# The opening of a fused attention-and-MLP kernel in a new order: first value products before first key products, value weights loaded earlier

## The chip, the cores and the metric

The kernel runs on one core of one Trainium2 chip. The metric is the device time of one execution in microseconds (us). The core has five engines that run at the same time, each through its own queue in order: TensorE (PE in the profile, its weight loads are PEld), VectorE (DVE), ScalarE (ACT), GpSimd (POOL) and SyncE (SP), which here only issues DMA transfers.

## The reference

One block with two halves over x, 2048 tokens by 512 features, in bfloat16. `c` is a condition vector; `mod` holds six vectors of 512 made from it.

```python
mod = (silu(c) @ w_mod)            # sa, ca, ga, sb, cb, gb
h = layernorm(x) * (1 + ca) + sa
q, k, v = h @ wqkv                 # 32 heads of 16
pq, pk = q @ w_phi, k @ w_phi      # per head, 16 x 16
phi_q = concat(softmax(pq), softmax(-pq)); phi_k likewise
kv = sum over tokens of phi_k^T v;  z = sum over tokens of phi_k
o = (phi_q @ kv) / (phi_q . z + 1e-6)
x = x + ga * (o @ wo)
h = layernorm(x) * (1 + cb) + sb
x = x + gb * ((sigmoid(h @ w_gate) * (h @ w_up)) @ w_down)
```

The sums kv and z run over all 2048 tokens, so no token's attention output can start before the last token's key features are in.

## The kernel before, in words

The tokens are 16 tiles (0 to 15) of 128. All weights stay in on-chip memory. `w_phi` is folded into the query and key weights, so that one product per tile gives pq or pk. The program is a graph of 1230 named tasks. Each task has an engine and issues one or a few instructions. One long string, `ORDER` (line 39 on), names every task once; a name may carry `@A`, `@D` or `@P`, which puts it on ACT, DVE or POOL. The string is emitted from front to back, so it sets the order of each engine's queue and, through the slots that it hands out, which buffer and which of the eight PSUM banks a task gets. Nothing reorders it later: an instruction that waits holds all that stands behind it in its queue.

The names that are needed below, with the lines of their instructions:

- `ld_x0a`, `ld_x0b`, `ld_x1a` and so on (L537, on SP) load two tiles of x each, 256 KB: x0a tiles 0 and 1, x0b 2 and 3, x1a 4 and 5, x1b 6 and 7, x2b 10 and 11; `ld_x3a` loads tiles 12 to 15. `ld_wk0`, `ld_wk1` (L545) load the halves of the key weights, 256 KB each. `ld_wm00a/b` and `ld_wm01a/b` (L542) load the four pieces of `w_mod` for sa and ca, 256 KB each: wm00 for the features of blocks 0 and 1, wm01 for blocks 2 and 3. `ld_wv0` (L551) loads the value weights, 512 KB.
- `st1_t` (L702 and L703, DVE) takes mean and variance of tile t; `rs1_g` (L709/L710 on ACT, L712/L713 on POOL) the inverse root for a group of one or two tiles; `nmr1_g` (L718, DVE) mean times it; `xn1_t` (L731 POOL, L729 DVE) normalizes; `tphgj` (L744, PE) transposes block j of group g.
- `c1`, `c2`, `c3` make silu(c). `modc1.0` and `modc1.1` (L630, PE) multiply it with wm00 and wm01, and `modc1c0` (ACT) and `modc1c1` (L638, DVE) copy the results out. `hm1_gj` (L751 ACT, L753 DVE or POOL) applies (1 + ca) and sa to block j of group g. Blocks 0 and 1 need modc1c0, blocks 2 and 3 need modc1c1. The result is `h1T`.
- `tpw`, `wTc`, `fold1`, `foldc1` (L661, L664, L679, L685) fold the key weights; `warm` (L600) are matrix products of zeros.
- `Kt` (L817) and `Vt` (L821) are the key and value products, four matmuls of 512 columns; the first ones are cut in halves `a` (blocks 0, 1) and `b` (blocks 2, 3). `et` (L776, ACT) takes both exponentials, `nt` (L780, DVE) their sums, `rt` (L794/L795 ACT, L798 DVE) the reciprocals, `phit` (L787, DVE or POOL) the features, `vat` (L836) copies the values out, and `kvt` (L282, PE) adds to the sums. `qe`, `qn`, `qphi` (L784) are the same for the queries.
- `kvn0`, `kvn1` (L294) and `kvz0`, `kvz1` (L299), on DVE, mask the finished sums. They wait for every `kvt`. After them come `num` (L326) and the attention output, the second normalization and the MLP, whose products (L447, L485) fill TensorE to the end.

[...]

Of the kernel before, what the change touches and what calls it, by code (L numbers as in the profile page):

```python
# [43 lines left out]
K1a hm1_20@A ld_x2a hm1_12 hm1_02@A wqT1 ld_x3a tph03 xn1_4 hm1_23 hm1_13@A tph41 st1_8 hm1_03@A hm1_41@A st1_9 K0a hm1_22@A rs1_6@P tph43 hm1_43@A tph40 K1b
rs1_5@P K0b ld_wv0 wqT3 tph30 tph33 tph32 K2a tph42 hm1_40 wqT2 fold01 hm1_33 tph31 nmr1_6 K2b ld_wmga st1_14 hm1_30@A xn1_11 e0.0 hm1_31@A wqT0 xn1_10 xT1_11
K3a xT1_10 K3b foldc01 nmr1_5 xn1_8 V3a st1_15 e3.0 V0a rs1_8@P e2.0 V0b V3b fold03 va3 foldc03 ld_wmm2 V2a st1_12 n0.0 V2b xn1_9 fold02 nmr1_8 r0.0@A hm1_32
modca.0 va0 foldc02 modca.1 tph50 n2.0 xn1_15 modcac hm1_50 n3.0 e1.0 xn1_14 phi0.0 hm1_60@P V1a V1b hm1_62@P K4a hm1_63@P fold00 tph82 tph52 K4b foldc00
r2.0@A va1 va2@D r3.0@A Q0 st1_13 rs1_7@P hm1_82@A n1.0 hm1_42@A kv0.0 Q2 Q1 r1.0@A phi3.0@D phi2.0@D modc2.0 qe0.0 modc2.1 nmr1_7 qe2.0 ld_wo xn1_12 phi1.0@D
tph51 qe1.0 modc2c xn1_13 qn0.0 e4.0 kv1.0 qn2.0 hm1_52 kv2.0 Q4 K5a kv3.0 xT1_12 xT1_13 qphi0.0@P qphi0.1@P qn1.0 qe4.0 qphi2.1 tph80 K5b hm1_80@A hm1_51@A
e5.0 pT0 qphi2.0 n4.0 r4.0@A qn4.0 n5.0 phi4.0@D qphi1.1@P hm1_61@P qphi1.0@P tph53 V5 K7a V4 va5 hm1_53@A V6 pT2 hm1_70@P qphi4.1 va4 hm1_71 mask4 va6 K6a  # L50
K7b K6b e6.0 K8 tph83 hm1_83 r5.0 qphi4.0@P e8.0 pT1 pT4 ld_wd2 tph81 hm1_81 n6.0 n8.0 e7.0 n7.0 V7 kv4.0 hm1_72@P K11 K9 V9 K14 V8 r6.0@A e9.0 va7 va9 r7.0@A
e11.2 e11.6 phi5.0 phi6.0 hm1_73@P n9.0 r9.0@A kv5.0 gwa gra gwb e11.4 e14.0 K10 phi7.0@D kv6.0 K12 V10 kv7.0 e14.4 r8.0 n11.6 n11.2 r11.6 phi9.0 e10.0 e12.0
ld_wd ld_wu0 grb n11.4 n14.0 r11.2 n14.4 r14.0 n10.0 r14.4@A phi8.0 va8 V11 V14 n12.0 e11.0 K13 n11.0 phi11.6 r11.4 wo1 r11.0 va10 r10.0@A va11 kv8.0 kv9.0
phi11.2@D phi11.0@D phi10.0@D phi11.4@D V12 K15 e13.0 wmod_free ld_wg0 phi14.4 phi14.0 kv10.0 kv11.4 kv11.6 Q6 kv11.0 e13.4 r12.0@A e15.4 n13.0 n13.4 r13.0
r13.4 n15.4 e15.0 va14 V15 V13 qe6.0 va12 kv11.2 n15.0 r15.0 r15.4@A va13 phi13.4 Q5 phi15.4 phi13.0@D va15 phi15.0@D phi12.0@D wo0 wo3 Q3 kv12.0 kv13.0
kv14.0 kv15.0 qn6.0 kvn0 kvz0 kv13.4 kv14.4 kv15.4 kvz1 kvn1 num0a num1a num2a wo2 rd0a wo_all rd1a qe3.0 u0a num0b num4a num1b rd0b Q11 qe5.0 rd2a u0b u2a
rd4a num2b qn3.0 u1a rd1b tpo0 Q8 qphi6.0@P qphi6.1@P oT0 out0 num4b rd2b u1b wd0 qe11.0 u2b qphi3.1@P qphi3.0@P x1_0 rd4b st2_0 qe8.0 Q7 qe7.0 tpo1 oT1 Q10
Q9 out1 Q15 oT2 rs2_0 qn5.0 nmr2_0 xn2_0 u4a u4b x1_1 qn7.0 tsw xnT0 out2 qphi5.1@P qphi5.0@P pT6 mod02 mod00 qphi7.0@P pT3 mod03@A mod01@A qe15.0 qphi7.1@P
Q13 g0.8 x1_2 tg0.8 g0.1 st2_1 wd1 rs2_1 tg0.1 u0.8 u0.1 g0.0 num3b g0.4 hm0.1 hm0.8 pT5 qe9.0 tg0.4 g0.9 wd2 u0.4 u0.9 rd3b u3b tg0.9 g0.5 num3a hm0.4 hm0.9
u0.2 u0.0 num6a tg0.5 tg0.0 rd3a u3a u0.5 g0.2 hm0.0 hm0.5 rd6a nmr2_1 qe10.0 tg0.2 oT4 g0.10 u0.10 wd6 hm0.2 g0.3 pT7 tg0.3 u6a g0.6 num6b u0.3 y0.0 y0.1  # L60
rd6b tg0.10 hm0.10 hm0.3 num5a num5b u6b rd5b wd3 wd4 wd5 oT3 oT6 xn2_1 qe13.0 tg0.6 rd5a y0.2 u5b g0.7 tg0.7 out4 u5a oT5 qn11.0 u0.6 u0.7 xnT1 num7a hm0.6
hm0.7 mod13@A mod12@A rd7a x1_4 y0.3 out3 qphi11.1@P qphi11.0@P x1_3 st2_3 out6 mod10@A mod11@A g1.2 tg1.2 g1.1 tg1.1 num7b wd7 u1.3 u1.2 hm1.2 u7a g1.4 u1.1
y0.4 rd7b hm1.1 u1.4 y0.5 tg1.4 hm1.4 g1.0 g1.10 u1.10 g1.3 u7b st2_2 rs2_2 tg1.10 tg1.3 hm1.10 hm1.3 pT11 out5 tg1.0 u1.7 g1.7 x1_6 nmr2_2 u1.0 hm1.0 g1.5
u1.5 x1_5 qn10.0 wd8 y0.6 g1.6 oT7 xn2_2 xn2_3 g1.8 y0.7 Q14 y0.8 wd10 tg1.7 tg1.5 hm1.5 out7 u1.8 u1.6 st2_4 tg1.6 xnT2 xnT3 wd9 x1_7 qphi10.0 Q12 hm1.7
st2_6 mod21@P mod20@P qphi10.1@P y1.0 pT10 tg1.8 mod22@A mod23@A hm1.6 g1.9 y1.1 y1.2 tg1.9 u1.9 y0.9 y1.3 y1.4 g2.5 y0.10 g2.6 st2_5 qe12.0 st2_7 hm1.8 qn9.0
tg2.5 qe14.0 rs2_4 hm1.9 rs2_3 nmr2_4 y1.5 u2.0 g2.1 g2.0 tg2.0 xn2_7@D hm2.0 nmr2_3 fin0 y1.6 g2.2 tg2.2 u2.6 u2.2 hm2.2 u2.1 num11b y1.7 g2.4 rd11b u11b
xn2_6@P xnT7 xnT6 u2.5 tg2.1 xn2_5 qphi9.1@P hm2.1 tg2.6 u2.8 xn2_4 hm2.5 g2.3 num11a rd11a u11a u2.9 qphi9.0@P xnT5 y1.8 xnT4 tg2.4 u2.4 hm2.4 hm2.6 tg2.3
# [991 lines left out]
```

## Time and profile before

| | |
|---|---|
| median of 3 runs | 204.66 us (203.75 to 204.67) |
| time of the profiled execution | 204.01 us |
| its span from first to last instruction | 202.3 us |
| busy PE / DVE / ACT / POOL | 195.3 / 160.1 / 105.1 / 104.7 us |
| masked key sums (first L294 on DVE) begin | 56.80 us |
| granted TensorE clock | 1.00 |

The span is shorter than the execution's time by 1.7 us that lie around it. Times in the trace count from the start of the span. In a timeline row stand start, duration, engine, line, operation, output and inputs, shape and count, and in brackets the idle time before it with what ended it. Durations of neighbours on one engine overlap by up to 0.1 us, so that the cost of an instruction in a full queue is the distance from its start to the next one's.

### The profile page before, as it was taken

To read this page: it belongs to the slowest core of one execution; us is meant where nothing else is said; L and a number is where in the kernel's file an instruction comes from. 1 tells how busy PE (TensorE), PEld (TensorE's weight loads), DVE (VectorE), ACT (ScalarE), POOL (GpSimd) and SP (SyncE) were. 2 spreads that over 40 slices of the span, in tenths; PEclk is the share of its full clock that TensorE was granted. 3 is DMA by queue.
4 is the path that set the end of the run, shared out by engine and by line. 5 is a ranking of instruction groups with operands and counts; after the bars stand their busy time and mean duration, and the time that the engine had idled before them with its cause. 6 is when DMAs were issued, how large, how long until landed. Compare 5 with 4: busy or idle time off the path is not lost.

```text
span 202.3 us, 4156 instructions
## 1 busy us (share of the span) xinstructions
PE 195.3 (97%) x1471; PEld 106.1 (52%) x1471; DVE 160.1 (79%) x374; ACT 105.1 (52%) x253; POOL 104.7 (52%) x147
## 2 busy tenths in 40 slices
...
GB/s 169 326 293 236 282 213 122 111 57 241 393 281 74 136 103 59 80 34 102 129 78 80 54 76 82 104 105 52 26 26 81 2 78 52 30 3 20 33 55 55
DMA packets 49452, 22.92 MB, mean 113 GB/s; under 512 B 38065, under 2 KB 47634, under 8 KB 49426
## 3 DMA queue, kind: packets, MB, share of 16 engines
...
q14 instruction: 14, 0.11, 0.2%
...
HBM read 11.58 MB, written 2.10 MB: 68 GB/s over the span
## 4 chain that ended last, share of the span: by engine, by line
PE 74%; DVE 7%; DMA 6%; ACT 5%; SPq 3%; issue 2%; POOL 1%; POOLq 0%; DVEq 0%; ACTq 0%
PE y_ps L485 19%; PE u_ps L447 18%; PE g_ps L447 17%; DMA wmod_sb<-in_w_mod_dram 6%; PE a_ps L356 6%; PE k_ps L817 3%; PE v_ps L821 3%; PE num L326 2%; PE q_ps L871 2%; ACT e L776 2%; DVE ks L780 2%; PE g_ps L449 1%; DVE qks L780 1%; SPq L537 1%; DVE phi L787 1%
## 5 line engine op out<-in xcount | busy, mean ns | idle before, releaser
L457 ACT ACTIVATE tg<-g_ps 128x512 bf16<-128x512 f32 (+5 forms) x66 | 28.9, 455 | 66.8 <-PE g_ps L447 39.7
L485 PE MATMUL y_ps<-wd_sb,wmod_sb 128*128 128x512 bf16 (+4 forms) x187 | 45.7, 367 | 0.0
L468 DVE SCALAR_TENSOR_TENSOR wmod_sb<-tg,u_ps 128x512 bf16<-128x512 bf16 (+4 forms) x63 | 30.3, 491 | 18.0 <-ACT tg L457 11.5
L447 PEld LDWEIGHTS <-wg_sb 128*128 128x128 bf16 (+1 forms) x252 | 21.9, 99 | 16.1
L447 PEld LDWEIGHTS <-wu_sb 128*128 128x128 bf16 (+1 forms) x252 | 21.8, 99 | 15.9 <-issue 0.3
L784 POOL TENSOR_TENSOR qphi<-qe,qks 128x512 bf16<-128x512 bf16 x24 | 25.1, 1061 | 4.2 <-DMA pT<-qphi 1.6
L485 PEld LDWEIGHTS <-wmod_sb 128*128 128x128 bf16 (+1 forms) x187 | 17.0, 97 | 16.0 <-issue 0.6
L447 PE MATMUL u_ps<-wT_sb,wu_sb 128*128 128x512 bf16 (+2 forms) x124 | 23.8, 322 | 0.0
L447 PE MATMUL g_ps<-wT_sb,wg_sb 128*128 128x512 bf16 (+2 forms) x124 | 23.1, 322 | 0.0
L447 PE MATMUL g_ps<-wqk_sb,wg_sb 128*128 128x128 bf16 (+4 forms) x128 | 20.0, 287 | 0.0
L447 PE MATMUL u_ps<-wqk_sb,wu_sb 128*128 128x128 bf16 (+4 forms) x128 | 19.8, 287 | 0.1
L376 POOL TENSOR_SCALAR ve<-mv 128x2 f32<-128x2 f32 (+1 forms) x8 | 1.8, 224 | 33.7 <-DVE mv L366 33.6
L492 DVE TENSOR_TENSOR ot<-y_ps,x 128x512 bf16<-128x512 f32 (+2 forms) x17 | 11.1, 654 | 10.2 <-PE y_ps L485 10.1
L780 DVE TENSOR_REDUCE qks<-qe 128x64 bf16<-128x1024 bf16 x16 | 19.2, 1204 | 0.0
L780 DVE TENSOR_REDUCE ks<-e 128x64 f32<-128x1024 bf16 (+2 forms) x22 | 19.1, 899 | 0.0
L776 ACT ACTIVATE e<-k_ps 128x512 bf16<-128x512 f32 (+2 forms) x44 | 18.0, 514 | 0.0
L776 ACT ACTIVATE qe<-q_ps 128x512 bf16<-128x512 f32 x32 | 17.1, 613 | 0.6 <-POOL phi L787 0.3
L817 PE MATMUL k_ps<-wqk_f,h1T 128*128 128x512 bf16 x64 | 16.6, 379 | 0.0
L871 PE MATMUL q_ps<-wqk_f,h1T 128*128 128x512 bf16 x64 | 15.9, 378 | 0.4 <-ACT wqk_f L685 0.4
L356 PE MATMUL a_ps<-wo_sb,oT 128*128 128x512 bf16 x64 | 16.3, 379 | 0.0
L787 POOL TENSOR_TENSOR phi<-e,kr 128x1024 bf16<-128x1024 bf16 (+2 forms) x10 | 14.4, 1446 | 3.3 <-ACT kr L795 2.1
L821 PE MATMUL v_ps<-wv_sb,h1T 128*128 128x512 bf16 x64 | 15.8, 379 | 0.2 <-ACT vaug L836 0.2
...
## 6 DMA issues: line engine op xcount, KB each, us to landing
...
x_sb<-in_A_x_dram SPq DMA_DIRECT2D x6, 256.0 KB, 4.7
...
wg_sb<-in_B_w_gate_dram SPq DMA_DIRECT2D x1, 1376.0 KB, 12.1
...
wmod_sb<-in_w_mod_dram SPq DMA_DIRECT2D x4, 256.0 KB, 6.1
wqk_sb<-in_A_wqkv_dram SPq DMA_DIRECT2D x2, 256.0 KB, 4.4
```

Source lines behind the costliest of these rows:

```text
L356: pe.matmul(ap_[:], lhsT=oT[:, j, :], rhs=wo_sb[:, j, :], start=(j == 0), stop=(j == KT - 1))
L447: pe.matmul(ps[:fsz, 0:n], lhsT=w[:, j, ft * P:ft * P + fsz], rhs=h[:, j, 0:n], start=(j == 0), stop=(j == KT - 1))
L457: G.add(f"tg{k}.{ft}", {"ACT": 0.13 + n * 0.00083}, lambda e, tg=tg, g_ps=g_ps, fsz=fsz, n=n: act.activation(tg[:fsz, 0:n], g_ps[:fsz, 0:n ...
L468: dve.scalar_tensor_tensor(hm_all[:fsz, hm[k].slot, ft, 0:n], tg[:fsz, 0:n], 1.0, u_ps[:fsz, 0:n], op0=ALU.add, op1=ALU.mult)
L485: mm = pe.matmul(y[:, 0:c1 - c0], lhsT=hm_all[:fsz, hm[k].slot, ft, tl * P:(tl + 1) * P], rhs=wd_sb[:fsz, ft, c0:c1], start=(ft == 0), sto ...
L776: act.activation(ee[:, a:b, s].rearrange("p g f h -> p g (f h)"), kp[:, a * 64:b * 64].rearrange("p (g n) -> p g n", n=64), ACT.Exp, scale ...
L780: dve.tensor_reduce(ks[:, a:b].rearrange("p g s h -> p (g s) h"), ee[:, a:b].rearrange("p g s f h -> p (g s) h f"), axis=AX.X, op=ALU.add)
L784: engine(e).tensor_tensor(ph[:].rearrange("p (g s f h) -> p g s f h", s=2, f=DH, h=4)[:, :, s], ee[:, :, s], ks[:, :, 1 - s].unsqueeze(2). ...
L787: engine(e).tensor_tensor(ph[:, a * P:b * P].rearrange("p (g f h) -> p g f h", f=DH, h=4), ee[:, a:b].rearrange("p g s f h -> p (g s) f h" ...
L817: pe.matmul(kp[:], lhsT=h1T[:, j, t * P:(t + 1) * P], rhs=wqk_f[:, j, D:2 * D], start=(j == 0), stop=(j == KT - 1))
L821: pe.matmul(vp[:], lhsT=h1T[:, j, t * P:(t + 1) * P], rhs=wv_sb[:, j, :], start=(j == 0), stop=(j == KT - 1))
L871: pe.matmul(qp[:], lhsT=h1T[:, j, t * P:(t + 1) * P], rhs=wqk_f[:, j, 0:D], start=(j == 0), stop=(j == KT - 1))
```

## The change

The string `ORDER` is another one up to the masked key sums; from `kvn0` on it is the same word for word. No task is added or removed, and the same 400 tasks stand ahead of `kvn0`. Eight tasks change engine: `r2.0`, `qphi0.1` and `r14.4` go to DVE, `hm1_81`, `r11.4` and `r13.0` from DVE to ACT, `qphi4.1` and `phi11.0` from DVE to POOL. The first lines:

```diff
-wdz warm0 c1 warm1_0 warm1_1 warm1_2 warm1_3 warm1_4 ld_x0b st1_3 st1_2 rs1_2 pmem ld_x0a c2 st1_1 ld_wk0 nmr1_2 tpw1 c3 rs1_1 ld_x1b wTc1 nmr1_1 st1_0 ld_wk1
...
+pmem ld_x0b wdz warm0 c1 ld_wk0 tpw0 wTc0 ld_x0a tpw1 warm1_0 ld_wk1 bd c2 st1_2 st1_3 rs1_2 st1_1 warm1_1 warm1_2 warm1_3 nmr1_2 rs1_1 ld_x1b wTc1 warm1_4
...
```

SyncE's queue at the start of the program, before. The rows are, in order, x0b and x0a, wk0, x1b, wk1, x1a, wm00b and wm00a, x2b, wm01b and wm01a, x2a:

```order
L537 DMA x_sb<-in_A_x_dram 128x2x512 x2
L545 DMA wqk_sb<-in_A_wqkv_dram 128x2x512
L537 DMA x_sb<-in_A_x_dram 128x2x512
L545 DMA wqk_sb<-in_A_wqkv_dram 128x2x512
L537 DMA x_sb<-in_A_x_dram 128x2x512
L542 DMA wmod_sb<-in_w_mod_dram 128x4x256 x2
L537 DMA x_sb<-in_A_x_dram 128x2x512
L542 DMA wmod_sb<-in_w_mod_dram 128x4x256 x2
L537 DMA x_sb<-in_A_x_dram 128x2x512
```

And now: x0b, wk0, x0a, wk1, x1b, wm00b and wm00a, wv0, x2b and x1a, wm01b and wm01a:

```order
L537 DMA x_sb<-in_A_x_dram 128x2x512
L545 DMA wqk_sb<-in_A_wqkv_dram 128x2x512
L537 DMA x_sb<-in_A_x_dram 128x2x512
L545 DMA wqk_sb<-in_A_wqkv_dram 128x2x512
L537 DMA x_sb<-in_A_x_dram 128x2x512
L542 DMA wmod_sb<-in_w_mod_dram 128x4x256 x2
L551 DMA wv_sb<-in_A_wqkv_dram 128x4x512
L537 DMA x_sb<-in_A_x_dram 128x2x512 x2
L542 DMA wmod_sb<-in_w_mod_dram 128x4x256 x2
```

The value weights move from behind x3a to the eighth place; x1a moves from sixth to tenth, behind them and x2b; x0a changes places with wk0.

VectorE's queue around `modc1c1` (L638), before. The first pair of rows is st1_4, the two pairs after L718 are st1_11 and st1_10:

```order
L702 BN_STATS st_81<-x_sb 128x6
L703 BN_AGGR mv_82<-st_81 128x2
L729 TENSOR_SCALAR xn<-x_sb,mv_82,rs_84 128x512
L718 TENSOR_SCALAR nmr<-mv_82,rs_84 128x1 x2
L702 BN_STATS st_81<-x_sb 128x6
L703 BN_AGGR mv_82<-st_81 128x2
L702 BN_STATS st_81<-x_sb 128x6
L703 BN_AGGR mv_82<-st_81 128x2
L718 TENSOR_SCALAR nmr<-mv_82,rs_84 128x1 x2
L638 TENSOR_TENSOR modc<-modc_ps,mone 128x2x2
L753 TENSOR_SCALAR h1T<-tp_h,modc 128x128
```

And now, where the first pair is st1_5 and the last is st1_10:

```order
L702 BN_STATS st_81<-x_sb 128x6
L703 BN_AGGR mv_82<-st_81 128x2
L729 TENSOR_SCALAR xn<-x_sb,mv_82,rs_84 128x512
L638 TENSOR_TENSOR modc<-modc_ps,mone 128x2x2
L718 TENSOR_SCALAR nmr<-mv_82,rs_84 128x1 x2
L753 TENSOR_SCALAR h1T<-tp_h,modc 128x128
L753 TENSOR_SCALAR h1T<-tp_h,modc 128x256
L702 BN_STATS st_81<-x_sb 128x6
L703 BN_AGGR mv_82<-st_81 128x2
```

The two statistics of tiles 10 and 11 that stood ahead of L638 now stand behind it. Ahead of it are, as before, those of tiles 0 to 7.

TensorE's queue behind the last matmul of `modc1.1`, where the first of the four long products stands; one piece of the difference, the lines with + being the new place of these rows (warm1_11, tph13 and tph00, V1a):

```order
 L630 MATMUL modc_ps<-sc_bf,wmod_sb 128x1
+L600 LDWEIGHTS wd_sb
+L600 MATMUL warm<-wd_sb 128x512
+L744 LDWEIGHTS xn
+L744 MATMUL tp_h<-ident,xn 128x128
+L744 LDWEIGHTS xn
+L744 MATMUL tp_h<-ident,xn 128x128
+L821 LDWEIGHTS h1T
+L821 MATMUL v_ps<-wv_sb,h1T 128x512
```

Before, K1a followed `modc1.1` after one pair of transposes. Now V1a is the first long product, and like K1a it stands behind `modc1.1`.

More of the change, by code (lines that the diff above doesn't have):

```diff
@@ L39 @@
 ORDER = """
-wdz warm0 c1 warm1_0 warm1_1 warm1_2 warm1_3 warm1_4 ld_x0b st1_3 st1_2 rs1_2 pmem ld_x0a c2 st1_1 ld_wk0 nmr1_2 tpw1 c3 rs1_1 ld_x1b wTc1 nmr1_1 st1_0 ld_wk1
-ld_x1a bd xn1_3 warm1_5 tpw0 wTc0 fold11 warm1_6 xn1_1 tpw2 foldc11 wTc2 st1_6 tph10 tph12 st1_7 tph11 ld_wm00b rs1_0@P tpw3 warm1_7 fold10 st1_5 xn1_2 wTc3
-tph13 fold12 warm1_8 warm1_9 ld_wm00a fold13 modc1.0 foldc10 foldc12 st1_4 rs1_4@P tph20 warm1_10 warm1_11 ld_x2b foldc13 modc1c0 hm1_11@A tph21 xn1_0
-hm1_10@A rs1_3@P tph02 tph01 ld_wm01b hm1_21@A ld_wm01a hm1_01@A nmr1_4 tph23 tph00 hm1_00@A st1_11 modc1.1 xn1_7 xn1_6 st1_10 nmr1_3 xn1_5 tph22 modc1c1@D
@@ L44 @@
[L44 to L67, printed above, removed]
@@ new lines @@
+tpw3 xn1_2 c3 wTc3 ld_wm00b warm1_5 st1_0 nmr1_1 warm1_6 fold10 warm1_7 ld_wm00a tpw2 ld_wv0 warm1_8 fold13 ld_x2b xn1_3 tph22 ld_x1a tph23 ld_wm01b foldc10
+ld_wm01a st1_7 st1_6 wTc2 tph21 ld_x2a fold11 warm1_9 foldc13 xn1_1 tph10 foldc11 wqT3 tph12 fold12 foldc12 modc1.0 modc1c0 warm1_10 tph20 tph11 st1_4 rs1_0@P
+rs1_4@P modc1.1 ld_x3a hm1_10@A wqT2 warm1_11 st1_5 xn1_0 modc1c1@D tph13 hm1_11@A tph00 V1a ld_wmga hm1_20@A nmr1_4 tph02 hm1_12 hm1_21@A tph03 hm1_23 ld_wo
+K3a tph01 hm1_13@A wqT1 wqT0 V1b hm1_00@A st1_10 hm1_22@A V3a hm1_03@A ld_wd2 hm1_02@A K3b hm1_01@A rs1_3@P xn1_7 xn1_6 tph43 nmr1_3 xn1_4 st1_11 tph42 tph40
@@ new lines @@
+st1_8 va1 tph41 K2a hm1_41@A hm1_40 K2b st1_9 st1_12 xn1_5 tph32 hm1_42@A rs1_6@P nmr1_6 tph31 e3.0 tph30 V3b va3 hm1_32 e2.0 rs1_5@P xn1_10 nmr1_5 xn1_9
+st1_15 K0a K0b e0.0 K1a tph33 hm1_31@A K1b xT1_10 xn1_11 xT1_11 V2a V0a V0b fold03 hm1_43@A st1_14 rs1_8@P V2b xn1_8 fold00 ld_wmm2 hm1_33 n0.0 nmr1_8 fold02
+modca.0 foldc03 modca.1 hm1_30@A fold01 va0 modcac xn1_15 va2@D foldc00 foldc02 foldc01 K4a xn1_14 tph51 tph50 K5a K4b K5b n2.0 hm1_60@P tph82 gwa tph80
+st1_13 r0.0@A hm1_63@P hm1_50 r2.0 n3.0 e1.0 phi0.0 hm1_51@A hm1_80@A Q1 qe1.0 V6 ld_wu0 Q2 r3.0@A hm1_62@P kv0.0 n1.0 phi2.0@D r1.0@A phi3.0@D hm1_82@A va6
@@ new lines @@
+Q4 Q0 tph52 phi1.0@D rs1_7@P nmr1_7 kv1.0 xn1_13 xT1_13 xn1_12 qn1.0 qphi1.1@P kv2.0 qe2.0 kv3.0 modc2.0 qphi1.0@P hm1_52 tph81 xT1_12 qn2.0 qe4.0 e4.0 K6a
+qn4.0 K6b hm1_81@A qe0.0 modc2.1 modc2c tph83 V4 qphi2.0 tph53 pT1 e5.0 hm1_53@A va4 qphi2.1 n4.0 n5.0 r4.0@A qn0.0 phi4.0@D K7a K7b V7 qphi4.1@P qphi4.0@P
+hm1_70@P hm1_71 hm1_61@P qphi0.1 va7 e7.0 pT2 V5 qphi0.0@P e6.0 pT4 K8 V9 r5.0 pT0 hm1_83 va9 kv4.0 V10 K9 va5 e8.0 n6.0 r6.0@A e9.0 n7.0 r7.0@A K14 K11 n8.0
+e11.6 phi5.0 kv5.0 V11 hm1_72@P phi6.0 hm1_73@P e11.4 e14.0 n9.0 K10 n11.6 r9.0@A kv6.0 phi7.0@D e11.0 r8.0 n14.0 e11.2 n11.2 n11.0 V8 gra kv7.0 phi9.0 e10.0
@@ new lines @@
+r11.6 n10.0 r11.2 va8 e14.4 K12 V12 va11 V14 n11.4 ld_wd va10 phi8.0 n14.4 phi11.6 kv8.0 kv9.0 r10.0@A r11.4@A K13 ld_wg0 r11.0 r14.0 e12.0 phi10.0@D mask4
+va14 kv10.0 r14.4 phi11.4@D phi11.2@D n12.0 e13.4 n13.4 e13.0 phi11.0 kv11.0 va12 kv11.4 kv11.6 K15 kv11.2 e15.0 r12.0@A n13.0 Q6 e15.4 gwb r13.4 r13.0@A
+phi14.4 V15 V13 n15.0 wo1 phi14.0 phi12.0@D n15.4 qe6.0 grb r15.4@A va13 r15.0 phi13.4 phi15.4 phi13.0@D Q3 kv12.0 phi15.0@D va15 Q5 wmod_free qn6.0 wo3
+kv13.0 wo0 kv14.0 kv15.0 kvn0 kvz0 kv13.4 kv14.4 kv15.4 kvz1 kvn1 num0a num1a num2a wo2 rd0a wo_all rd1a qe3.0 u0a num0b num4a num1b rd0b Q11 qe5.0 rd2a u0b
@@ new lines @@
+u2a rd4a num2b qn3.0 u1a rd1b tpo0 Q8 qphi6.0@P qphi6.1@P oT0 out0 num4b rd2b u1b wd0 qe11.0 u2b qphi3.1@P qphi3.0@P x1_0 rd4b st2_0 qe8.0 Q7 qe7.0 tpo1 oT1
+Q10 Q9 out1 Q15 oT2 rs2_0 qn5.0 nmr2_0 xn2_0 u4a u4b x1_1 qn7.0 tsw xnT0 out2 qphi5.1@P qphi5.0@P pT6 mod02 mod00 qphi7.0@P pT3 mod03@A mod01@A qe15.0
+qphi7.1@P Q13 g0.8 x1_2 tg0.8 g0.1 st2_1 wd1 rs2_1 tg0.1 u0.8 u0.1 g0.0 num3b g0.4 hm0.1 hm0.8 pT5 qe9.0 tg0.4 g0.9 wd2 u0.4 u0.9 rd3b u3b tg0.9 g0.5 num3a
+hm0.4 hm0.9 u0.2 u0.0 num6a tg0.5 tg0.0 rd3a u3a u0.5 g0.2 hm0.0 hm0.5 rd6a nmr2_1 qe10.0 tg0.2 oT4 g0.10 u0.10 wd6 hm0.2 g0.3 pT7 tg0.3 u6a g0.6 num6b u0.3
@@ new lines @@
+rd10a hm2.9 qphi8.0@P u2.10 pT9 y2.1 y2.2 y2.3 y2.4 y2.5 qn14.0 num9b rd9b qphi13.0 qphi8.1@P mod30@A mod33@A tg2.10 mod40@A y2.6 y2.7 g3.3 wr qphi13.1@P
+tg3.3 oT11 g3.0 u10a rd10b u10b pT8 oT10 hm2.10 qn15.0 g3.8 num9a rd9a u9a u3.0 out11 y2.8 g3.1 y2.9 qphi14.1 fin1 x1_11 u9b u3.3 hm3.3 st1 tg3.8 tg3.0 u3.8
+num8a st2_11 num8b rd8b rd8a u8a pT13 qphi15.0 hm3.8 u8b u3.9 g3.4 u3.2 out10 x1_10 qphi14.0 oT8 oT9 hm3.0 st2_10 y2.10 g3.6 u3.6 qn12.0 rs2_6 out8 tg3.4
+tg3.6 x1_8 hm3.6 nmr2_6 st2_8 xn2_11@P qphi15.1@P u3.4 g3.9 tg3.9 hm3.9 u3.1 g3.5 qphi12.1@P out9 fin2 g3.2 tg3.2 hm3.4 tg3.1 x1_9 st2_9 g3.7 y3.0 y3.1 y6.0
```

41 lines of the change are left out of this document (22 added, 19 removed).

## The prediction

> **What bounds the kernel now.** I read the busy time by stretch first, cut where the first key products begin, where the masked key sums begin, and where the MLP fills TensorE. Columns: stretch, its length, then busy time with instruction count of PE, PEld, DVE, ACT and POOL, granted clock, DMA share, GB/s.
>
> ```profile
> core 0: us, PE busy (x) PEld busy (x) DVE busy (x) ACT busy (x) POOL busy (x), PEclk, DMA share, GB/s
> 13.20:56.80 43.60, 42.93 (x395) 23.54 (x393) 42.59 (x86) 42.10 (x117) 37.58 (x43) 1.00 0.89 218
> 56.80:69.00 12.20, 11.70 (x111) 6.68 (x108) 12.02 (x34) 10.56 (x23) 12.04 (x12) 1.00 0.52 139
> 69.00:202.27 133.27, 129.93 (x877) 70.17 (x874) 96.15 (x226) 43.75 (x95) 45.32 (x63) 1.00 0.33 63
> ```
>
> In the stretch that the change rewrites three engines are full at once: PE, DVE and ACT each idle 0.7 to 1.5 us of 43.6. From 56.80 to 69 DVE is still full, and then PE to the end. Next I asked what DVE ever waited for between 4 and 57 us, in total, times and longest:
>
> ```profile
> DVE st L702 <- DMA x_sb<-in_A_x_dram: 2.5, 1, 2.5
> DVE nmr L718 <- POOL rs L713: 0.6, 1, 0.6
> ```
>
> The 2.5 us are the wait before its first statistics at 3.72. After that there is one gap of 0.6 us until the masked sums at 56.80. So VectorE is a gapless queue of 53 us, and the sums cannot begin before it has worked through. No reordering can shorten such a queue by more than the 0.6 us; only work moved to other engines can. What can lengthen it is a wait. The timeline of DVE gives its fixed points:
>
> ```profile
> 3.72 0.69 DVE L702 BATCH_NORM_STATS2 st<-x_sb 128x6 f32<-128x512 bf16 x1 [2.53 <-DMA x_sb<-in_A_x_dram]
> ...
> 5.34 0.66 DVE L702 BATCH_NORM_STATS2 st<-x_sb 128x6 f32<-128x512 bf16 x1
> ...
> 9.36 0.66 DVE L702 BATCH_NORM_STATS2 st<-x_sb 128x6 f32<-128x512 bf16 x1
> ...
> 11.25 0.33 DVE L718 TENSOR_SCALAR nmr<-mv,rs 128x1 f32<-128x1 f32 x2
> 11.49 0.68 DVE L702 BATCH_NORM_STATS2 st<-x_sb 128x6 f32<-128x512 bf16 x1
> ...
> 13.10 0.30 DVE L718 TENSOR_SCALAR nmr<-mv,rs 128x1 f32<-128x1 f32 x2
> 13.32 0.15 DVE L638 TENSOR_TENSOR modc<-modc_ps,mone 128x4 f32<-128x4 f32 x1
> ...
> 56.80 0.43 DVE L294 TENSOR_TENSOR kvb<-kvacc,mask 128x256 bf16<-128x256 f32 x1
> ```
>
> By the order of its queue, 5.34 is st1_1 (needs x0a), 9.36 is st1_5 with st1_4 behind it (both need x1a), xn1_0 follows and ends at 11.25, and 13.32 is modc1c1.
>
> **When the loads land.** The chain of waits (start, length) and the timeline of PEld show two landings, the busy time by stretch the rate between them, and the list of DMA issues the sizes:
>
> ```profile
> 6.54 6.08 DMA wmod_sb<-in_w_mod_dram
> ```
>
> ```profile
> 5.87 0.39 PEld L661 LDWEIGHTS <-wqk_sb 128*128 128x128 bf16 x4 [0.36 <-DMA wqk_sb<-in_A_wqkv_dram]
> ```
>
> ```profile
> 3.72:9.36 5.64, 5.16 (x46) 2.99 (x46) 5.36 (x18) 3.63 (x11) 4.15 (x7) 1.00 1.13 317
> 9.36:13.51 4.15, 3.47 (x56) 2.18 (x53) 3.98 (x15) 4.12 (x12) 3.62 (x7) 1.00 1.23 285
> ```
>
> ```profile
> x_sb<-in_A_x_dram SPq DMA_DIRECT2D x6, 256.0 KB, 4.7
> ...
> wv_sb<-in_A_wqkv_dram SPq DMA_DIRECT2D x1, 512.0 KB
> ```
>
> Every load up to wm01a is of 256 KB like those of x here. Before, wk0 is the third and lands at 5.87, and wm01a is the eleventh and lands at 12.62. The DMA engines are full all the way (shares of 1.13 and 1.23), and the rate is 285 to 317 GB/s. So a load's landing is set by the bytes that stand ahead of it. The 512 KB of wv0 take 524 KB / 317 = 1.65 us to 524 / 285 = 1.84 us; I take 1.7.
>
> **The change part by part.** *x0a* is now third, so it lands at 5.87, where wk0 did. DVE is ready for st1_1 at 5.34: a wait of 0.5.
>
> *x1a* is the tenth load, but wv0 counts double, so 11 x 256 KB have to land up to it, as many as landed by 12.62. I take 12.6. DVE has the statistics of tiles 0 to 3, 6 and 7 and the small steps done when it did before, 9.36, plus 0.5: 9.9. It then waits 2.7 us for st1_4, and everything behind it waits too: the queue is in order, and no work that could be done earlier stands ahead.
>
> *wm01a* lands 1.7 after 12.62, at 14.3. Its matmuls started at 12.66 (row in the rivals); from there to modc1c1 took 13.32 - 12.66 = 0.66, so modc1c1 can start at 15.0. DVE, with st1_4, st1_5 and xn1_0 (11.25 - 9.36 = 1.9 us) behind it, gets there at 12.6 + 1.9 = 14.5: a wait of 0.5. Before there was none, because st1_11, st1_10 and an nmr (13.32 - 11.49 = 1.8 us) filled that time; now these come after.
>
> Sum of new waits: 0.5 + 2.7 + 0.5 = 3.7 us. As a check, modc1c1 starts at 15.0 and not at 13.32, and 1.8 us of work and one nmr (0.2) that were done by then are not: 1.7 + 2.0 = 3.7.
>
> *The old gap* of 0.6 us came from rs1_7 on POOL. Its nmr now stands one phi later on DVE. I credit the whole 0.6; the bounds are 0 and 0.6.
>
> *Tasks that change engine.* Forms on DVE up to 57 us: line, shapes, count, busy us, mean ns.
>
> ```profile
> L753 DVE TENSOR_SCALAR h1T<-tp_h,modc 128x256 bf16<-128x256 bf16 x8 | 3.0, 391 | 0.0
> L798 DVE RECIPROCAL kr<-ks 128x32 bf16<-128x32 f32 x4 | 1.2, 326 | 0.1
> L784 DVE TENSOR_TENSOR qphi<-qe,qks 128x512 bf16<-128x512 bf16 x3 | 1.2, 417 | 0.0
> L798 DVE RECIPROCAL kr<-ks 128x64 bf16<-128x64 f32 x2 | 1.1, 540 | 0.0
> L787 DVE TENSOR_TENSOR phi<-e,kr 128x256 bf16<-128x256 bf16 x3 | 0.8, 303 | 0.0
> L798 DVE RECIPROCAL kr<-ks 128x16 bf16<-128x16 f32 x4 | 0.8, 224 | 0.0
> ```
>
> DVE loses hm1_81 (0.39), qphi4.1 (0.42), r11.4 (0.22), phi11.0 (0.30) and r13.0 (0.33), in all 1.66, and gains r2.0 (0.54), qphi0.1 (0.42) and r14.4 (0.33), in all 1.29. As neighbours overlap, the difference is worth 0.2 to 0.4: a gain of 0.3.
>
> *Value products first.* V1a stands behind modc1.1 on PE, whose matmuls now start at 14.3 and not at 12.66. So the first long product comes about 1.7 us later than K1a did, and having wv0 early does not help it. *ACT* loses less than DVE: it can do blocks 0 and 1 of tiles 1 to 3 before it stops for modc1c1, and DVE's end is the later one. *wo, wd2 and wu*, also issued earlier, I cost at nothing. wo's 512 KB (1.7 us) go out while SyncE would only wait for POOL's normalized tiles 10 and 11, which are late by DVE's delay; without that cover the second load of w_mod, and modc2 with it, would be 1.7 later. wu (1376 KB, some 4.6 us at 300 GB/s) lands ahead of the transposes of tiles 12 and 13, whose key products are among the last on PE; if they came up sooner, they would wait those 4.6.
>
> Sum at kvn0: 3.7 - 0.6 - 0.3 = +2.8 us. From there the order is the same, DVE is full for 12.02 of 12.20 us and PE for 129.93 of 133.27, so nothing takes the delay up: I carry it over whole. The profiled execution took 204.01 us (span 202.3 and 1.7 around it), so 206.8; it lies 0.65 below the median of 204.66, from which the same sum gives 207.5. I forecast between them: **207.2 us**. Its own range: 1.65 or 1.84 for wv0, the old gap kept or not, and up to 1 us for stalls further on: 206.2 to 208.5.
>
> **Rivals.** *The TensorE clock drops.* Timeline of PE:
>
> ```profile
> 4.11 2.10 PE L600 MATMUL warm<-wd_sb 128*128 128x512 bf16 x5
> ...
> 10.10 0.55 PE L630 MATMUL modc_ps<-sc_bf,wmod_sb 128*128 128x1 bf16 x16
> ...
> 12.66 0.55 PE L630 MATMUL modc_ps<-sc_bf,wmod_sb 128*128 128x1 bf16 x16 [0.56 <-DMA wmod_sb<-in_w_mod_dram]
> ...
> 13.19 0.59 PE L817 MATMUL k_ps<-wqk_f,h1T 128*128 128x512 bf16 x2
> ```
>
> Five products of 512 columns took 2.10 us (0.42 each) in the beginning; later two take 0.59 including the last one's tail, about half as long each. Now only some 0.5 us of work stands between modc1.0 (about 10.7) and modc1.1 (14.3), so PE idles about 3 us where it idled 0.56. If that sends it back to half speed for as long as at the start (until 4.11 + 2.10 = 6.2 at the latest; I take 4.6 us of it), PE loses another 2.3 us in a stretch in which it is full too; 1.7 + 2.3 less the 0.7 it idled before is 3.3, against DVE's 2.8, and where the two queues wait for each other some of both: +3.8, 208.2. For it speaks the length of the gap, against it that the clock stayed up over 0.56. [...]
>
> *TensorE sets the end and VectorE makes its waits good.* PE is as full as DVE (42.93 of 43.60). If the masked sums follow from PE's queue alone, its delay of 1.7 less 0.7 of idle time is +1.0 at most, and +0.3 if the waits further on vanish too: about 205.1. Against it: DVE must still do 56.80 - 9.36 less 0.9, some 46.5 us of work, after x1a.
>
> *x1a and wm01a land on time.* One mechanism, at the DMA engines: if they moved wv0's 512 KB beside the others without slowing them, x1a would land by 9.9 and wm01a by 12.6, and DVE would wait 0.5 and save 0.9: -0.4, so 204.1, not slower. The point at which it turns is x1a at about 10.3. Against it speaks that 285 to 317 GB/s at full shares left no room; from the first landing (3.72) to wm01a's ten loads came in 8.9 us, 295 GB/s; to have x1a at 10.3 they would need 6.6 us, a third faster.
>
> *Later stalls pile up:* ACT and POOL meet a DVE that is 3 us late and hold it up in turn. Among ACT's waits before stands one of this kind:
>
> ```profile
> ACT ks L794 <- DVE ks L780: 0.5, 1, 0.5
> ```
>
> Three such waits would give 208.7. Against it: all of DVE's inputs come later by its own delay or less.
>
> **How the numbers follow.** VectorE starved 0.70, clock 0.08, later stalls 0.08: slower. TensorE alone 0.09: most of it within 0.5% (1.0 us, about what a measurement of this kernel can tell from no change). Loads on time 0.05: same, or a little faster. So faster 0.03, same 0.11, slower 0.86. The range of 205.4 to 208.8 leaves out about a tenth on either side.
>
> **What would show it.** In the changed kernel's timeline, an L702 on DVE that ends an idle time of over 2 us released by DMA x_sb near 12.6; L638 near 15.0; L294 near 59.6; the gap at L718 gone. If x1a's statistics start before 10.5, or L294 comes before 57.5, the reasoning is wrong; if L638 is late but L294 is not, DVE was not the bound.

## The result and the profile after

| | before | after |
|---|---|---|
| median of 6 runs each, on the same chip | 204.39 us (203.54 to 204.82) | 209.42 us (208.56 to 210.24) |
| ratio, 95% interval | | 1.0249 [1.0212, 1.0285] |
| the profiled execution, its span | 204.01 us, 202.3 us | 209.25 us, 207.2 us |
| masked key sums begin (first L294 on DVE) | 56.80 us | 61.38 us |
| granted TensorE clock | 1.0 | 0.992 |

The change made the kernel slower, as forecast, but by 5.0 us and not by 2.8. 209.42 lies above the range that was given, and the size has to be explained.

The busy time by stretch of the changed kernel, cut where the last matmuls of `modc1.1` begin, at the masked key sums and 12.2 us later (columns as before):

```profile
14.06:61.38 47.32, 45.40 (x407) 24.94 (x415) 45.10 (x91) 43.69 (x120) 40.03 (x47) 0.96 0.83 211
61.38:73.58 12.20, 11.55 (x108) 6.65 (x107) 12.02 (x34) 10.19 (x23) 12.04 (x12) 1.00 0.32 61
73.58:207.17 133.59, 129.19 (x862) 70.23 (x873) 96.24 (x226) 43.68 (x95) 45.42 (x63) 1.00 0.33 63
```

What follows the masked sums takes 12.20 + 133.59 = 145.8 us and took 12.20 + 133.27 = 145.5. Nearly the whole loss is made ahead of them: 61.38 - 56.80 = 4.58 of the span's 4.9 us. What is new in the first row is the granted clock of 0.96.

What DVE waited for between 4 and 62 us of the changed kernel (in total, times, longest):

```profile
DVE st L702 <- DMA x_sb<-in_A_x_dram: 5.3, 3, 2.3
DVE h1T L753 <- PE tp_h L744: 1.0, 1, 1.0
DVE modc L638 <- PE modc_ps L630: 0.4, 1, 0.4
DVE ks L780 <- POOL qphi L784: 0.3, 1, 0.3
DVE qks L780 <- ACT kr L795: 0.2, 1, 0.2
```

Before, this table had two rows, the 2.5 us ahead of the first statistics and the 0.6 at L718. The second is gone. In its place stand two more waits for x, one for `modc_ps`, one for `tp_h`, and two small ones far behind. The timeline of DVE tells where:

```profile
3.53 0.70 DVE L702 BATCH_NORM_STATS2 st<-x_sb 128x6 f32<-128x512 bf16 x1 [2.34 <-DMA x_sb<-in_A_x_dram]
...
5.93 0.69 DVE L702 BATCH_NORM_STATS2 st<-x_sb 128x6 f32<-128x512 bf16 x1 [0.69 <-DMA x_sb<-in_A_x_dram]
...
12.30 0.69 DVE L702 BATCH_NORM_STATS2 st<-x_sb 128x6 f32<-128x512 bf16 x1 [2.24 <-DMA x_sb<-in_A_x_dram]
...
14.69 0.16 DVE L638 TENSOR_TENSOR modc<-modc_ps,mone 128x4 f32<-128x4 f32 x1 [0.38 <-PE modc_ps L630]
...
19.31 0.41 DVE L753 TENSOR_SCALAR h1T<-tp_h,modc 128x256 bf16<-128x256 bf16 x1 [1.00 <-PE tp_h L744]
...
61.38 0.41 DVE L294 TENSOR_TENSOR kvb<-kvacc,mask 128x256 bf16<-128x256 f32 x1
```

x0a is there at 5.93, x1a at 12.30, and `modc1c1` starts at 14.69. These three are the waits that were forecast, 0.69 + 2.24 + 0.38 = 3.3 us in all. The fourth, at 19.31, was not in the sum. TensorE's timeline shows where it comes from:

```profile
11.11 0.35 PE L744 MATMUL tp_h<-ident,xn 128*128 128x128 bf16 x3
14.06 0.59 PE L630 MATMUL modc_ps<-sc_bf,wmod_sb 128*128 128x1 bf16 x16 [2.60 <-DMA wmod_sb<-in_w_mod_dram]
14.51 0.59 PE L600 MATMUL warm<-wd_sb 128*128 128x512 bf16 x1
...
15.32 0.63 PE L821 MATMUL v_ps<-wv_sb,h1T 128*128 128x512 bf16 x1
...
16.39 1.06 PE L817 MATMUL k_ps<-wqk_f,h1T 128*128 128x512 bf16 x2
...
18.26 0.59 PE L817 MATMUL k_ps<-wqk_f,h1T 128*128 128x512 bf16 x2
```

TensorE stood 2.60 us for the second load of w_mod, and the work after that ran at half speed: two key products took 1.06 us at 16.39 and 0.59 at 18.26. The busy time by stretch, cut at the changes of the granted clock:

```profile
10.62:14.03 3.41, 0.79 (x12) 0.30 (x9) 1.66 (x5) 2.30 (x7) 0.59 (x1) 1.00 1.35 301
14.03:17.45 3.42, 3.11 (x26) 1.74 (x28) 2.97 (x13) 1.98 (x5) 3.23 (x5) 0.50 1.03 283
17.45:20.86 3.41, 3.41 (x28) 1.99 (x27) 2.34 (x7) 2.54 (x6) 1.88 (x5) 1.00 1.54 262
```

From 14.03 to 17.45 the clock is 0.50, just behind 3.41 us in which TensorE was busy for 0.79. At half speed those 3.42 us hold 1.7 us less work, the transposes came late, and VectorE stood for them at 19.31.

### The profile page after: what moved, and what is told of

Its sections match the earlier page's. It is cut to its first block, busy times and chain, and to the rows that moved or that the text cites. A ratio compares the mean times of both kernels' runs of the same rounds, so it can differ in the third digit from the quotient of the medians.

```text
span 207.2 us, 4138 instructions
## 1 busy us (share of the span) xinstructions
PE 196.1 (95%) x1447; PEld 107.3 (52%) x1471; DVE 160.9 (78%) x372; ACT 105.8 (51%) x254; POOL 105.3 (51%) x148
## 4 chain that ended last, share of the span: by engine, by line
PE 67%; ACT 10%; DMA 8%; DVE 6%; issue 3%; POOL 3%; SPq 1%; ACTq 0%; DVEq 0%
PE y_ps L485 18%; PE u_ps L447 17%; PE g_ps L447 17%; PE a_ps L356 5%; ACT e L776 4%; DMA wmod_sb<-in_w_mod_dram 3%; PE num L326 2%; DMA wp_sb<-in_A_w_phi_dram 2%; ACT qe L776 2%; PE k_ps L817 2%; DMA pT<-qphi 2%; DMA h1T<-xn 2%; DVE ks L780 1%; ACT vaug L836 1%; PE g_ps L449 1%
## 5 line engine op out<-in xcount | busy, mean ns | idle before, releaser
L485 PE MATMUL y_ps<-wd_sb,wmod_sb 128*128 128x512 bf16 (+4 forms) x180 | 44.2, 366 | 0.2
L780 DVE TENSOR_REDUCE ks<-e 128x64 f32<-128x1024 bf16 (+2 forms) x22 | 19.1, 906 | 0.3 <-POOL qphi L784 0.3
L780 DVE TENSOR_REDUCE qks<-qe 128x64 bf16<-128x1024 bf16 x16 | 19.2, 1204 | 0.2 <-ACT kr L795 0.2
L787 POOL TENSOR_TENSOR phi<-e,kr 128x1024 bf16<-128x1024 bf16 (+2 forms) x11 | 15.4, 1410 | 2.4 <-DVE phi L787 1.6
```

The lines of the kernel that those rows point to most:

```text
L485: mm = pe.matmul(y[:, 0:c1 - c0], lhsT=hm_all[:fsz, hm[k].slot, ft, tl * P:(tl + 1) * P], rhs=wd_sb[:fsz, ft, c0:c1], start=(ft == 0), sto ...
L780: dve.tensor_reduce(ks[:, a:b].rearrange("p g s h -> p (g s) h"), ee[:, a:b].rearrange("p g s f h -> p (g s) h f"), axis=AX.X, op=ALU.add)
L787: engine(e).tensor_tensor(ph[:, a * P:b * P].rearrange("p (g f h) -> p g f h", f=DH, h=4), ee[:, a:b].rearrange("p g s f h -> p (g s) f h" ...
```

## The experiments

My theory after the result: VectorE's queue is delayed by what lands late (x0a, x1a, wm01a), by some 3 us as forecast, and the half clock on TensorE adds the rest. The rivals were that x1a's wait alone is the cost, that the order of the products is, that the rest is lost to the order further on, and that the transposes come late behind `modc1.1` whatever the clock is. In the diffs only the words that move are shown; they are the words of the order, and loads are issued in the order in which they stand.

### The loads alone: the kernel before, with the new order of its first 13 loads

```diff
-ld_x0b ld_x0a ld_wk0 ld_x1b ld_wk1 ld_x1a ld_wm00b ld_wm00a ld_x2b ld_wm01b ld_wm01a ld_x2a
+ld_x0b ld_wk0 ld_x0a ld_wk1 ld_x1b ld_wm00b ld_wm00a ld_wv0 ld_x2b ld_x1a ld_wm01b ld_wm01a ld_x2a
```

> The kernel before with nothing but the first thirteen loads in the changed kernel's order. If the loads set it: VectorE waits 0.5 to 0.7 us for x0a and 2.2 us for x1a as in the changed kernel; modc1c1, which here has 1.8 us more work ahead of it, comes near 16; the time rises by 2.5 to 4 us to 207 to 208.5. If the order of the instructions is at fault, it stays at 204.4 within 0.7.

It took 207.95 us (206.87 to 208.87), ratio 1.0193 [1.0144, 1.0243]. DVE's waits in this kernel:

```profile
DVE st L702 <- DMA x_sb<-in_A_x_dram: 5.4, 3, 2.7
DVE h1T L753 <- PE tp_h L744: 1.5, 1, 1.5
```

`modc1c1` came at 16.41. The order of the loads alone, with key products first, costs 3.9 us of the 5.0, and value products first are not needed for it. But its profiled execution was at half speed for 6.83 us, twice as long as the changed kernel's. Three of its four runs have a mean clock of 0.98 and took 207.90 to 208.87 us; the fourth has 0.992, like the changed kernel's profile, and took 206.87, nearer to 3 us above the kernel before.

### The value weights behind w_mod: the changed kernel, wv0 issued behind wm01a

```diff
-ld_wm00a ld_wv0 ld_x2b ld_x1a ld_wm01b ld_wm01a ld_x2a
+ld_wm00a ld_x2b ld_x1a ld_wm01b ld_wm01a ld_wv0 ld_x2a
```

> The changed kernel with one transfer moved: the value weights go out behind wm01a instead of ahead of x2b, x1a, wm01b and wm01a. If the loads set it (my theory): x1a then lands about 1.5 us earlier, near 10.8, and wm01a near 12.5, so VectorE's wait for x_sb falls from 2.2 to about 0.7 us, modc1c1 comes near 13.2 instead of 14.69, TensorE idles 1.2 us instead of 2.8 ahead of modc1.1 and keeps its full clock (no half-speed stretch in the record, and no wait of VectorE for tp_h). The masked sums come 2.5 to 3.5 us earlier than in the changed kernel and the time is 205.5 to 207. If the order of the instructions is at fault and not the loads, the time stays within 0.7 us of the changed kernel's 209.4.

It took 208.26 us (208.19 to 208.48), ratio 1.0212 [1.0175, 1.025]. That was a miss: most of the gain did not come. x1a now ended a wait of only 0.69 us, and `modc1c1` came 1.0 earlier (13.69). But now V1a, which stands ahead of the transposes in TensorE's queue, waited for its own weights, and the clock fell to half here too. Timeline of PE, and busy time by stretch:

```profile
13.10 0.55 PE L630 MATMUL modc_ps<-sc_bf,wmod_sb 128*128 128x1 bf16 x16 [1.33 <-DMA wmod_sb<-in_w_mod_dram]
...
14.53 0.39 PE L821 MATMUL v_ps<-wv_sb,h1T 128*128 128x512 bf16 x1 [0.31 <-DMA wv_sb<-in_A_wqkv_dram]
```

```profile
11.72:15.14 3.42, 1.67 (x24) 0.99 (x25) 2.97 (x11) 2.47 (x7) 1.97 (x5) 1.00 1.23 242
15.14:18.55 3.41, 3.41 (x12) 1.19 (x10) 2.07 (x8) 2.07 (x5) 3.00 (x5) 0.50 1.12 328
```

VectorE's wait for `tp_h` grew from 1.00 to 1.85 us:

```profile
19.17 0.41 DVE L753 TENSOR_SCALAR h1T<-tp_h,modc 128x256 bf16<-128x256 bf16 x1 [1.85 <-PE tp_h L744]
```

A part of the gain was lost elsewhere: VectorE waited 1.19 us for x0a in this execution, not 0.69, with the same loads ahead of it. So with the value products first neither of these two places for wv0 is free: ahead of w_mod it delays `modc1.1`, behind it it delays the first product.

### x1a in time: the changed kernel, x1a ahead of wv0

```diff
-ld_wv0 ld_x2b ld_x1a ld_wm01b ld_wm01a
+ld_x1a ld_wv0 ld_x2b ld_wm01b ld_wm01a
```

> The changed kernel with x1a ahead of the value weights; the pieces of w_mod land when they did. If VectorE is held by whatever lands last, x1a or wm01a (my theory): its wait for x_sb near 10 goes, but it then stands at modc1c1 until 14.7 as before, some 2.5 us, because nothing else stands ahead of it: the time stays at 209.4 within 0.5. If the wait for x1a is what the change cost: 2.2 us come back, 207.2.

It took 209.26 us (208.29 to 210.24), ratio 1.026 [1.0201, 1.0318], no change. The wait of 2.24 us for x1a is gone from DVE's timeline, and another of 2.70 stands at the next late thing:

```profile
14.45 0.16 DVE L638 TENSOR_TENSOR modc<-modc_ps,mone 128x4 f32<-128x4 f32 x1 [2.70 <-PE modc_ps L630]
...
19.17 0.41 DVE L753 TENSOR_SCALAR h1T<-tp_h,modc 128x256 bf16<-128x256 bf16 x1 [1.10 <-PE tp_h L744]
```

The rival that x1a's wait alone is the cost is out. What sets `modc1c1` is wm01a, which lands behind the same bytes in either order.

### Only the end of w_mod late: the kernel before, wv0 ahead of wm01b and wm01a

```diff
-ld_x2b ld_wm01b ld_wm01a ld_x2a ld_x3a ld_wv0
+ld_x2b ld_wv0 ld_wm01b ld_wm01a ld_x2a ld_x3a
```

> The kernel before with the value weights ahead of wm01b and wm01a, and nothing else moved; x1a and all other loads that VectorE needs stay early. If modc1c1 is what holds the queues (my theory after the run with x1a ahead): wm01a lands near 14.1, VectorE stands at modc1c1 for 1.2 to 1.6 us, and TensorE idles about 2.1 us ahead of modc1.1, so that its clock may halve for one window: 1.3 to 2.8 us slower, 205.3 to 206.8. If only loads of x count: 204.0 within 0.5.

It took 205.84 us (204.75 to 207.25), ratio 1.0109 [1.0069, 1.015]. DVE's timeline:

```profile
14.30 0.16 DVE L638 TENSOR_TENSOR modc<-modc_ps,mone 128x4 f32<-128x4 f32 x1 [1.00 <-PE modc_ps L630]
...
18.45 0.41 DVE L753 TENSOR_SCALAR h1T<-tp_h,modc 128x256 bf16<-128x256 bf16 x1 [1.36 <-PE tp_h L744]
```

Here, as in the experiment before it, x1a is early and wm01a late, and `modc1c1` starts at nearly the same time (14.30 and 14.45). But VectorE stands 1.00 us instead of 2.70, because in the old order the statistics of tiles 11 and 10 stand ahead of L638 and fill 1.7 us.

### The clock held up: zero products ahead of modc1.1

`warm1_11`, one product on zeros that feeds nothing, becomes several and moves directly ahead of `modc1.1`, into the time in which TensorE idles. Three kernels: the changed one with 12 of them (e3), the changed one with 7 (e9), and the one just shown, wm01 late (e6), with 8 (e8). Nothing of the computation is left out.

```diff
-warm(f"warm1_{i}", 1, 0.22, r=["c1"], w=["warm"])
+warm(f"warm1_{i}", 12 if i == 11 else 1, 0.22, r=["c1"], w=["warm"])
...
-modc1.1 ... warm1_11
+warm1_11 modc1.1
```

> The changed kernel with twelve products of zeros on TensorE directly ahead of modc1.1, in the time in which it would idle (11.3 to 14.06); nothing else moves. If the idle time halved the clock and the half clock cost time: no half-speed stretch between 14 and 17.4 us in the record, VectorE's wait of 1.0 us for tp_h near 18.3 is gone, and the time falls by 1.0 to 1.5 us to 207.9 to 208.4. If the wait for tp_h comes from the order of TensorE's queue and the clock costs nothing: 209.4 within 0.5.

With 12 it took 208.03 us (207.69 to 208.92), ratio 1.0206 [1.0163, 1.0249]: 1.4 below the changed kernel, as expected, though the two intervals overlap. But its profiled execution was the slowest of its four: the clock rose only at 10.66, not at 7.21, TensorE was behind, and the zeros themselves delayed `modc1.1`. DVE's waits show that trade:

```profile
DVE st L702 <- DMA x_sb<-in_A_x_dram: 4.8, 2, 2.6
DVE modc L638 <- PE modc_ps L630: 2.5, 1, 2.5
```

The wait for `tp_h` is gone, and one of 2.5 us for `modc_ps` stands there. That profile could not tell the price of the clock, so I ran it again with fewer zeros.

> The changed kernel with 7 zero products directly ahead of modc1.1, where e3 had 12; at full clock they are 1.5 us, so that also after a cold start they delay modc1.1 less than e3's did. Mine: the half clock costs VectorE's 1.0 us at tp_h and some 0.3 to 0.4 further on, so 207.8 to 208.3, the waits for x_sb (about 3.0 in all) and modc_ps (0.4) unchanged, kvn0 near 60.2. If the clock halves all the same, because 1.5 us of work in the idle stretch are too little: 209 to 209.6. If the clock stays up and the time is still 209 or more, the wait at tp_h was not the clock.

With 7 it took 207.68 us (207.41 to 207.87), ratio 1.0184 [1.0166, 1.0203], and the clock was 1.0 in the profiled execution. Timeline of PE (six of the seven zero products make one row), then DVE's waits, then its timeline:

```profile
12.46 1.67 PE L600 MATMUL warm<-wd_sb 128*128 128x512 bf16 x6
14.21 0.55 PE L630 MATMUL modc_ps<-sc_bf,wmod_sb 128*128 128x1 bf16 x16
...
15.61 0.59 PE L817 MATMUL k_ps<-wqk_f,h1T 128*128 128x512 bf16 x2
```

```profile
DVE st L702 <- DMA x_sb<-in_A_x_dram: 5.4, 3, 2.7
DVE modc L638 <- PE modc_ps L630: 0.4, 1, 0.4
```

```profile
3.85 0.69 DVE L702 BATCH_NORM_STATS2 st<-x_sb 128x6 f32<-128x512 bf16 x1 [2.67 <-DMA x_sb<-in_A_x_dram]
...
5.81 0.69 DVE L702 BATCH_NORM_STATS2 st<-x_sb 128x6 f32<-128x512 bf16 x1 [0.25 <-DMA x_sb<-in_A_x_dram]
...
12.43 0.70 DVE L702 BATCH_NORM_STATS2 st<-x_sb 128x6 f32<-128x512 bf16 x1 [2.49 <-DMA x_sb<-in_A_x_dram]
...
14.80 0.16 DVE L638 TENSOR_TENSOR modc<-modc_ps,mone 128x4 f32<-128x4 f32 x1 [0.36 <-PE modc_ps L630]
...
59.73 0.41 DVE L294 TENSOR_TENSOR kvb<-kvacc,mask 128x256 bf16<-128x256 f32 x1
```

The waits for the loads are all there (0.25 + 2.49 + 0.36 = 3.1), the wait for `tp_h` is gone, and the two small waits at L780 with it. The masked sums begin at 59.73, which is 1.65 us before the changed kernel's 61.38 and 2.93 behind the old one's 56.80.

> The kernel before with wv0 ahead of the last two loads of w_mod, as in e6 (205.84 us, 1.0109; VectorE stood 1.00 us for modc_ps and 1.36 us for tp_h), and 8 zero products of TensorE directly ahead of modc1.1, some 1.7 us of work in the idle time there. Mine: the wait for tp_h is the half clock alone; with TensorE busy the clock stays up, that wait goes, and only modc_ps's wait of about 1.0 us and the closed or kept small gap remain: 204.3 to 205.0, no half clock between 13 and 20 us. Rival: tp_h is late because the transposes stand behind the late modc1.1 whatever the clock: 205.5 to 206.2, with the wait of 1.2 to 1.4 still there.

With 8 zeros in the kernel with the late wm01 it took 204.87 us (204.68 to 204.97), ratio 1.004 [1.0026, 1.0055], against 1.0109 without them. DVE's waits:

```profile
DVE modc L638 <- PE modc_ps L630: 1.5, 1, 1.5
```

There is no wait for `tp_h` any more. In both pairs it went with the half clock, although `modc1.1` came no earlier (14.28 on PE here, 13.71 without the zeros; 14.21 and 14.06 in the other pair). So the rival that the transposes are late whatever the clock is out.

A profile shows one execution, and full speed begins at another time in each (last section), so the runs have to bear this out. One stretch of 3.41 us at half speed takes 1.7 / 206 = 0.008 off a run's mean clock. All six runs of the changed kernel have 0.992 or less, all eight with zeros 0.996 or more. The kernel with wm01 late gives the pair even without zeros: one of its four runs kept its clock (1.000) and took 204.75 us, like the five runs with zeros (204.68 to 204.97), and the three at 0.992 took 205.67 to 207.25. Even of the kernel before one run in 31 beside these experiments has 0.992, and it took 205.22.

### The order further on: the old first 154 tasks, then the new order

The first 154 words of the old order, up to about 20 us, loads included; behind them the remaining words in the new order and on the new engines.

```diff
-(the new order's opening)
+pmem ld_x0b ld_x0a ld_wk0 ... va3 (the old order's first 154 words)
```

> The order of the kernel before for the first 154 tasks, up to some 20 us (its loads, its first key products and then the first value products), and behind them the remaining tasks in the changed kernel's order and on its engines. If the changed opening alone costs the time: 203.5 to 204.7, level with the kernel before, and no wait of VectorE for x_sb or tp_h. If the order further on costs by itself (VectorE waited 0.5 us around 40 us and one phi took 1.1 us instead of 0.7 there): 205 to 205.7.

It took 204.89 us (204.39 to 205.11), ratio 1.0052 [1.0038, 1.0066], between the two expectations. DVE's timeline and the row of one feature product:

```profile
21.73 0.69 DVE L836 CAST vaug<-v_ps 128x512 bf16<-128x512 f32 x1 [0.84 <-PE v_ps L821]
...
49.29 1.11 DVE L787 TENSOR_TENSOR phi<-e,kr 128x1024 bf16<-128x1024 bf16 x1
```

The 0.84 us lie close behind the seam at 20 us, and the changed kernel has no such wait; I take it that value products that the new order has early meet a front that has them late, which was not tried. So this run does not measure the order further on by itself. It does show that without the new opening 4 of the 5 us are gone.

### The old gap closed: the kernel before, nmr1_7 one phi later

```diff
-modc2.1 nmr1_7 qe2.0 ld_wo xn1_12 phi1.0@D tph51
+modc2.1 qe2.0 ld_wo phi1.0@D nmr1_7 xn1_12 tph51
```

> The kernel before with nmr1_7 one place later on VectorE, behind phi1.0, so that VectorE does not stand idle for rs1_7 (its one gap, 0.6 us at 27.4). If VectorE's gapless queue sets the masked sums: they come 0.4 to 0.6 us earlier and the time falls by as much, ratio 0.997 to 0.998. If TensorE and ScalarE, which are as full, set it too: less than 0.2 us, ratio 0.999 to 1.001.

It took 203.49 us (203.19 to 204.0, 12 runs) beside 203.9 (17 runs), ratio 0.9986 [0.9976, 0.9996]. DVE's waits and its first masked sum:

```profile
DVE st L702 <- DMA x_sb<-in_A_x_dram: 2.5, 1, 2.5
```

```profile
56.19 0.43 DVE L294 TENSOR_TENSOR kvb<-kvacc,mask 128x256 bf16<-128x256 f32 x1
```

The gap is gone and the masked sums begin 0.61 us earlier, as expected for a bound by VectorE's queue; of it only 0.3 to 0.4 us show in the time, which lies between the two expectations. It is the one version here whose interval lies below the kernel before, if by 0.1%.

## Why the prediction was right in direction and wrong in size

The terms of the sum, against DVE's timeline of the changed kernel and of the one with 7 zeros, whose clock stayed up:

| term at the masked sums, us | predicted | after | after, clock held |
|---|---|---|---|
| first statistics (x0b) earlier or later | 0 | -0.19 | +0.13 |
| wait for x0a | 0.5 | 0.69 | 0.25 |
| wait for x1a | 2.7 | 2.24 | 2.49 |
| wait for `modc_ps` | 0.5 | 0.38 | 0.36 |
| old gap at L718 | -0.6 | -0.6 | -0.6 |
| tasks that change engine, and the rest | -0.3 | +0.5 to +0.6 | +0.3 |
| wait for `tp_h` | not in the sum | 1.00 | none |
| small waits at L780 | not in the sum | 0.5 | none |
| start of the masked sums | +2.8 | +4.58 | +2.93 |

The rest row is what the other rows leave of the last one.

**Right:** that VectorE's queue bounds this part, so that its waits add up. That the loads land by the bytes ahead of them: x1a at 12.30 (12.6 forecast), `modc1c1` at 14.69 (15.0). That the gap at L718 goes. That nothing behind takes the delay up: the 4.58 us at the masked sums are 4.9 at the end of the span. With the clock held, the sum itself came out, +2.93 for +2.8, but in part by luck: the four rows of loads make 3.2 us where 3.7 were forecast, and the tasks that change engine cost 0.3 where 0.3 was credited.

*Value products first* was costed at the delay of `modc1.1`; V1a came at 15.32, 2.1 us after K1a's 13.19 and not 1.7; a zero product and two transposes stand between `modc1.1` and it, and they ran at half speed. *ACT* lost more than I said, 3.4 us for transposes:

```profile
ACT h1T L751 <- PE tp_h L744: 3.4, 3, 2.5
```

It stayed behind VectorE as the bound all the same: from 14.06 on it is busy for 43.69 of 47.32 us, VectorE for 45.10. *wo, wd2 and wu* cost nothing that shows: with the clock held VectorE waits for nothing but x and `modc_ps` ahead of the masked sums, and what follows them kept its length to 0.3 us. (wu's 1376 KB are 1409 kB, so at 300 GB/s 4.7 us and not 4.6.)

**Wrong: the step "The TensorE clock drops".** It stood among the rivals with a chance of 0.08 and a price of +1.0 on top of the sum. The sum was made without it, and the range ended at 208.8, little above the 208.2 of this rival. The gap that it named came as described, 2.60 us of idle time ahead of `modc1.1`, and the clock did fall. I had set it aside since the clock had stayed up over 0.56 us, which says little of a gap of 2.6. That it would stay up over a gap of some 3 us too was assumed, and no trace shows it; the falls here came behind gaps of 1.33 us (wv0 behind w_mod) to 2.60 (last section). The price was too low too. I had set TensorE's own delay, 3.3 us, beside VectorE's 2.8 and taken 3.8 for both; but on VectorE the two come one after the other: it had already waited out the loads when it met the late transposes, so that wait of 1.00 us was added whole, and half a us of small waits came behind it. Measured at the masked sums it is 61.38 - 59.73 = 1.65 us; by the ratios, 1.0249 and 1.0184 of about 204.3 us, it is 1.3 us, and between the medians 1.7. With it alone the forecast would have been 207.2 + 1.65 = 208.9; the rest of the way to 209.42 is in the next points.

**Mis-sized: "Tasks that change engine".** The credit of 0.3 is not to be seen. One instruction eats it: the product of phi10.0 on DVE (L787, 128x1024) takes 1.10 us in both kernels of the table and 1.11 in the spliced one, where the old kernel's group has a mean of 0.686:

```profile
53.19 1.10 DVE L787 TENSOR_TENSOR phi<-e,kr 128x1024 bf16<-128x1024 bf16 x1
```

Why it is longer was not tried. GpSimd was at products of the same line then (50.69 to 53.75), but also around the one at 58.14 (57.14 to 59.71), which took 0.67. Without its 0.42 the row with the clock held would be -0.1.

**Missing: 0.35 us around the span.** The profiled execution of before has 204.01 - 202.3 = 1.7 us outside its span, that of after 209.25 - 207.2 = 2.05. It is in every run, see the last section.

So of 5.24 us between the two profiled executions the forecast sum explains 2.9, the half clock 1.65, the time around the span 0.35, and some 0.3 behind the masked sums remain without a name.

**The other rivals.** *TensorE sets the end* is out, since with the clock held VectorE's waits came through to the masked sums (+2.93). *x1a and wm01a land on time* is out by the rows at 12.30 and 14.69. *Later stalls* is out as an independent cause: in the kernels with the new order the small waits at L780 were there with the half clock and not without it.
